# The row of token 512 on GpSimd instead of ScalarE, in an FNet and PEER kernel

## The chip, the core and the metric

The kernel runs on one core of a Trainium2 chip. Its engines run side by side, each in the order of its own queue: TensorE (PE in the profile; its weight loads are PEld), VectorE (DVE), ScalarE (ACT), GpSimd (POOL), and SyncE (SP), whose queue here issues nearly all the DMA transfers. An instruction starts when those before it on its engine have gone ahead and the semaphores that it waits for have come. The time is that of the whole program on the device, in microseconds, and the median of several runs counts. A profile is taken of one execution; it shows every instruction with its start and its length.

## The reference

`x` has 2048 tokens of 512 values. With `xn` the layer norm of `x`, the output is `x + A(xn) + B(xn)`:

```python
# A: Fourier mixing
a = einsum("bsd,ed->bse", x, dft_hid_re)
b = einsum("bsd,ed->bse", x, dft_hid_im)
y = einsum("ts,bse->bte", dft_seq_re, a) - einsum("ts,bse->bte", dft_seq_im, b)
# B: product-key experts, 32 heads, 64 x 64 experts
q = einsum("nd,dhc->nhc", xf, w_q)        # two halves q1, q2 per head
s1, s2 = q1 @ k1.T, q2 @ k2.T             # the best 2 of each, then the best 2 of the 4 sums
g = softmax(top_s); ue, ve = u[top_e], v[top_e]
act = gelu(einsum("nd,nhkd->nhk", xf, ue))
out = einsum("nhk,nhk,nhkd->nd", g, act, ve)
```

## The kernel before

**Stages.** The first 57 us or so hold the layer norm, the sequence transform of part A and the preparation of the query matrices. After them PE works through the scores of part B (line 776), the expert matmuls (905 and 988) and some small products, without using anything of the first stage but its results in memory.

**Groups and folds.** The host has reordered the tokens into four groups `g` of four blocks `q` of 128 tokens, taken in the order `G = (1, 0, 2, 3)`. A transform over 2048 tokens has mirrored columns and rows, so tokens are added to and subtracted from their mirror images before any matmul. `ln(g, n)` normalises group `g`: DVE (or ACT, for the blocks in `onact`) takes mean and variance; ACT takes a square root (316); DVE makes `rstd` and `negm` from it (317 to 321); ACT, and for group 1 DVE too, applies them (333). `fold(k, g)` then folds the group on DVE: `ft` (366), in `fold_d` `ff` and `fo` (348 to 355), and `Q[k][g]` (369, 370). One small copy of `fold_d` is on ACT (353). `main(k, g)` multiplies the DFT matrix by `Q[k][g]` on PE (400) and adds up over the four groups. `k` is 0 for the cosine and 1 for the sine half. `evict(0)` empties the sums of the cosine half out of PSUM (455) and adds the bias `s5c` to the first of them on the way.

**Token 512.** One token is its own mirror image in a way that the blocks have no place for. It is handled as one row on partition 0, `x5`, of two times 512 values:
- line 336 normalises it on GpSimd, when group 0's statistics are there;
- `fold_row(k)` folds it on GpSimd, into `s5` (k = 0) and `s5i` (k = 1), through the row tile `r` of tag `r5` and the same `fold_d`, with GpSimd as engine `e`;
- `spread()` multiplies `s5` by the two values `c52` (385), stores the four rows of 128 in memory and loads them back as columns `s5c` (386, 387: DMAs that GpSimd issues);
- `sides()` adds `s5` times a scalar to two side sums on partition 0 (435 to 438);
- `c52` (514) is a copy of two values of the row `c5r`, which a DMA loads at the start.

**What sets the order.** The program text gives dependences and a first order; each engine's instructions are then put in a queue of their own, by when a scheduler expects their data. So line 435, which stands late in the text, is issued as soon as `s5` is expected. In the queue of ACT the row's operations stand between those of `ln` and `fold`. The two places that the prediction speaks of, in the order of ACT's queue (the number is the line):

```
514 c52 <- c5r, 316 root of group 1, 333 apply x2, 353 copy of the fold of group 1, 297 ... statistics of group 0
333 apply group 0 x4, 353 row copy, 435 row * s5, 296, 385 row * c52 x2, 436 row * c55, 316 root of group 2
```

Of the kernel before, what the change touches and what calls it, by code (L numbers as in the profile page):

```python
# [8 lines left out]
F32 = mybir.dt.float32  # L9
# [6 lines left out]
AF = mybir.ActivationFunctionType  # L16
ALU = mybir.AluOpType
AX = mybir.AxisListType

P = 128  # L20
# [15 lines left out]
def tile_fnet_peer(ctx, tc, x, ca, cb, c5, wt, wf, wr, wq, kt, ut, vn, out):  # L36
# [9 lines left out]
    nc = tc.nc  # L46
# [202 lines left out]
    da = stA.enter_context(tc.tile_pool(name="da", bufs=1, side="left"))  # L249
# [6 lines left out]
    s5 = da.tile([1, 257], F32, name="s5")  # L256
# [9 lines left out]
    def row512(k, dst, eng=nc.sync):  # L266
        eng.dma_start(dst.rearrange("p (k c) -> p k c", k=4),
                      cb[k, 0, 4 * k:4 * k + 4, 0:1, 6:8].rearrange("k p b c -> p k (b c)"))
# [70 lines left out]
    def fold_d(k, t, f, o, e=nc.vector):  # L339

        op, po = (ALU.subtract, ALU.add) if k else (ALU.add, ALU.subtract)

        def halves(v):
            return v.rearrange("p q (s c) -> p q s c", s=2)

        e.tensor_tensor(halves(f)[..., 1:P], halves(t[:, :, 0:256])[..., 0:P - 1],
                          halves(t[:, :, 256:512])[..., 1:P], op=op)
        c = 256 - P * k  # L350
        e.tensor_tensor(o[:, :, c:c + 1], t[:, :, 127:128], t[:, :, 384:385], op=op)
        if k == 0:
            nc.scalar.activation(f[:, :, 0:P + 1:P], t[:, :, 255:257], AF.Copy)
        e.tensor_tensor(o[:, :, k:P], f[:, :, k:P], f[:, :, P + k:], op=op)
        e.tensor_tensor(o[:, :, P + k:2 * P], f[:, :, k:P], f[:, :, P + k:], op=po)

    def fold(k, g):


        op = ALU.subtract if k else ALU.add  # L360
        t = FF["t"] = da.tile([P, 2, 512], F32, tag="ft", name=f"ft{k}_{g}", bufs=1)
        f = None if k else FT.get(G.index(g))
        if f is None:
            f = da.tile([P, 2, 256], F32, tag="ff", name=f"ff{k}_{g}", bufs=2)
        o = FF[k, g] = da.tile([P, 2, 257], F32, tag="fo", name=f"fo{k}_{g}", bufs=2)
        nc.vector.tensor_tensor(t, xp[2 * g], xp[2 * g + 1], op=op)  # L366
        fold_d(k, t, f, o)
        c = slice(k, 257 - k)
        nc.vector.tensor_tensor(Q[k][g][:, 0, c], o[:, 0, c], o[:, 1, c], op=ALU.add)
        nc.vector.tensor_tensor(Q[k][g][:, 1, c], o[:, 0, c], o[:, 1, c], op=ALU.subtract)  # L370

    def fold_row(k):

        r = da.tile([1, 1, 768], F32, tag="r5", name=f"r5_{k}", bufs=1)
        nc.gpsimd.tensor_tensor(r[:, 0, 0:512], x5[:, 0], x5[:, 1], op=ALU.subtract if k else ALU.add)
        fold_d(k, r[:, :, 0:512], r[:, :, 512:768], (s5i if k else s5).unsqueeze(1), nc.gpsimd)

    s5_d = dram.tile([4, P], F32, name="s5_d")
    s5p = da.tile([1, 2, 2, P], F32, name="s5p")
    s5c = da.tile([P, 2, 2], F32, name="s5c")  # L380

    def spread():

        for a in range(2):
            nc.scalar.activation(s5p[:, a].rearrange("o t p -> o (t p)"), s5[:, 0:256], AF.Copy, scale=c52[:, a:a + 1])
        nc.gpsimd.dma_start(s5_d.rearrange("n p -> (n p)").unsqueeze(0), s5p.rearrange("o a t p -> o (a t p)"))
        nc.gpsimd.dma_start(s5c.rearrange("p a t -> p (a t)"), s5_d.rearrange("n p -> p n"), allow_slow_non_contiguous=True)

# [13 lines left out]
    def add(dst, a, v, first=False):  # L402

        if first:
            nc.vector.tensor_scalar(dst, v, a, None, op0=ALU.mult)
        else:
            nc.vector.scalar_tensor_tensor(dst, v, a, dst, op0=ALU.mult, op1=ALU.add)

    def halved(v):
        return v.rearrange("p (k q c) -> p k q c", q=2, k=4)  # L410

    def turned(v):
        return v.rearrange("p (q k c) -> p k q c", q=2, k=4)

    def sides():


        f = FF["t"][:, 0, 0:4]
        nc.vector.tensor_copy(f[:, 0:2], Q[0][G[0]][:, :, 256])
        nc.vector.tensor_copy(f[:, 2:4], c5s[:, :, G[0]])  # L420
        for n, g in enumerate(G):
            for h in range(2):
                a, v = Q[0][g][:, h, 256:257] if n else f[:, h:h + 1], A[0, g][:, h * 512:(h + 1) * 512]
                if n < 3:
                    add(s256[:, h], a, v, n == 0)
                    continue
                for q in range(2):
                    nc.vector.scalar_tensor_tensor(turned(a256[:, h])[:, :, q], halved(v)[:, :, q], a,
                                                   halved(s256[:, h])[:, :, q], op0=ALU.mult, op1=ALU.add)
        for n, g in enumerate(G):  # L430
            for k in range(2):
                add(a5[:, k, :257 - k], c5s[:, k, g:g + 1] if n else f[:, 2 + k:3 + k],
                    Q[k][g][:, k, :257 - k], n == 0)
        r = da.tile([1, 2, 512], F32, name="r256")
        nc.scalar.activation(turned(r[:, 0]), halved(c5r), AF.Copy, scale=s5[:, 256:257])
        nc.scalar.activation(r[:, 1, 0:257], s5, AF.Copy, scale=c55)
        nc.gpsimd.tensor_tensor(a256[0:1, 0], a256[0:1, 0], r[:, 0], op=ALU.add)
        nc.gpsimd.tensor_tensor(a5[0:1, 0], a5[0:1, 0], r[:, 1, 0:257], op=ALU.add)

# [70 lines left out]
    c52 = cst.tile([1, 2], F32, name="c52")  # L510
    c5r = da.tile([1, 512], F32, name="c5r")
    c55 = da.tile([1, 1], F32, name="c55")
    row512(0, c5r, nc.scalar)
    nc.scalar.activation(c52, c5r[:, 0:2], AF.Copy)
    nc.scalar.dma_start(c55, cb[0, 0, 0, 0:1, 8, 0:1])
    for g in G:
        load(1, g)
# [7 lines left out]
    for n, g in enumerate(G):  # L525
        if n < 2:
            ln(g, n)
        if 0 < n < 3:
            ln(G[n + 1], n + 1)
        fold(0, g)  # L530
        if n == 3:
            fold_row(0)
            spread()
            fold_row(1)
        main(0, g)
        if n == 0:
            for t in range(2):
                m_mul(0, t, (2, 3))
            for t in range(2, 4):
                m_mul(0, t, range(KD))  # L540
# [5 lines left out]
    for n, g in enumerate(G):  # L546
# [5 lines left out]
        if n:  # L552
            for q in range(4):
                xpose(4 * G[n - 1] + q, n < 3)
    sides()
    evict(1)
    for q in range(4):
# [754 lines left out]
    with tc.If(rv > 0):  # L1312
        with tc.tile_pool(name="gen", bufs=1) as gp, \
# [10 lines left out]
            def gload(src, shape, tag, name):  # L1324
                t = gp.tile(shape, F32, tag=tag, name=name, bufs=2)
                nc.sync.dma_start(t, src)
                return t

            gx = []
            for i in range(NT):  # L1330
                t = gload(x[i % 4, i // 4], [P, D], "x", f"gx{i}")
                norm(t, t, i)
                gx.append(gsplit(t, [P, D], "xs", f"gxs{i}", bufs=NT))
            for q in range(4):
                ya = gp.tile([P, 4, D], F32, tag="ya", name=f"gya{q}")
                for ri in range(2):
                    pp = [gps.tile([P, 512], F32, tag="gp", name=f"gp{q}{ri}{d}", bufs=4)
                          for d in range(KD)]
                    for i in range(NT):
                        t = gp.tile([P, 512], F32, tag="c", name=f"gc{q}{ri}{i}", bufs=2)  # L1340
# [15 lines left out]
                    for kd, pieces in enumerate((((0, 1, P, 0), (P - 1, 0, 1, 2)), ((0, 1, P, 1), (P - 1, 0, 1, 0)),  # L1356
                                                 ((0, 0, 1, 1), (1, 1, P, 2)), ((0, 0, P, 3),))):
                        t = gp.tile([P, 512], F32, tag="c", name=f"gw{q}{ri}{kd}", bufs=2)
# [3 lines left out]
                    for a in range(4):  # L1362
# [12 lines left out]
                        o = gload(out[b * P:(b + 1) * P], [P, D], "o", f"go{b}")  # L1375
# [54 lines left out]
```

## Time and profile before

| | us |
|---|---|
| median of 3 runs (1165.53 to 1167.51) | 1165.57 |
| the profiled execution | 1163.72 |
| its span, first to last instruction | 1161.9 |
| busy in the span: PE | 1135.6 |
| busy in the span: DVE | 933.6 |
| busy in the span: ACT | 614.6 |
| busy in the span: POOL | 238.2 |

Times inside the execution are counted from the start of the span. In rows of instructions in order of time the columns are start, length, engine, line and operation, then what it writes and reads, the shapes, and how many instructions are merged in the row; the brackets give the engine's idle time before it and what ended it. A row that merges several instructions gives the start of the first and the time that they were busy together. "ACTq" and "SPq" are the queues' own steps, such as issuing a DMA. In rows of windows, each engine has its busy time in that window and, in brackets, the number of instructions; then come the granted clock of PE (1.00 is full), the share of the DMA engines in use and GB/s.

### The profile page before, as it was taken

What the parts mean: (1) busy time and instruction counts of PE and PEld (TensorE: products, weight loads), DVE (VectorE), ACT (ScalarE), POOL (GpSimd) and SP (SyncE); (2) the same over time, 40 slices, a digit from 0 to 9 for tenths busy, and PEclk for the clock granted to TensorE, in tenths of its full rate; (3) what the DMA queues carried; (4) which work ended last, traced back from release to release, by engine and by line L of the source; (5) the groups of instructions that cost most, each with busy time, mean ns of one, the idle gap of its engine ahead of it and who ended that gap; (6) DMA issues with size and microseconds to landing.
All of it is one profiled execution on the core that took longest, in us unless ns stands there. A gap on an engine that the chain in (4) does not pass through costs nothing.

```text
span 1161.9 us, 25370 instructions
## 1 busy us (share of the span) xinstructions
PE 1135.6 (98%) x9930; PEld 724.4 (62%) x9930; DVE 933.6 (80%) x2840; ACT 614.6 (53%) x1063; POOL 238.2 (21%) x226
## 2 busy tenths in 40 slices
PE   5899999999999999999999999999999999999997
PEld 4355555445445449778478469569569559658763
DVE  5987889798998999983994895797886887788670
ACT  4684677777876645354435436436526436334440
POOL 4131455765756420000000010010010000000000
PEclk9899999999999999999999999999999999999999
DMA  9073345233341204261652743644545555451423
GB/s 364 28 265 99 119 132 178 82 146 117 102 146 41 89 25 129 73 217 28 226 174 98 233 157 127 195 163 158 185 158 173 167 173 168 155 170 56 140 74 103
DMA packets 81504, 163.64 MB, mean 141 GB/s; under 512 B 16084, under 2 KB 31323, under 8 KB 81374
## 3 DMA queue, kind: packets, MB, share of 16 engines
q1 hardware_dynamic: 81008, 161.84, 41.7%
q8 instruction: 80, 1.31, 0.5%
q14 instruction: 50, 0.41, 0.1%
q10 hardware_dynamic: 302, 0.08, 0.0%
q0 software_dynamic: 64, 0.00, 0.0%
HBM read 142.69 MB, written 17.63 MB: 138 GB/s over the span
## 4 chain that ended last, share of the span: by engine, by line
PE 94%; DVE 2%; ACT 1%; POOL 1%; DMA 1%; issue 0%; ACTq 0%
PE z L905 29%; PE s L776 29%; PE v L988 28%; PE g L943 4%; PE m L144 2%; PE p L400 2%; ACT xq L333 1%; DMA c5r<-in_cb_dram 1%; PE xp L472 0%; DVE L L933 0%; DVE ft L366 0%; POOL x L336 0%; DVE act L959 0%; DVE w L951 0%; PE hy L485 0%
## 5 line engine op out<-in xcount | busy, mean ns | idle before, releaser
L905 PE MATMUL z<-xb,u 128*128 128x256 f16 (+1 forms) x3840 | 342.7, 251 | 0.0
L988 PE MATMUL v<-v,act 128*128 128x512 f16 x1536 | 338.6, 379 | 0.0
L905 PEld LDWEIGHTS <-u 128*128 128x128 f16 x3840 | 309.7, 98 | 26.4
L776 PE MATMUL s<-m,xq 128*128 128x512 f16 x1344 | 297.3, 379 | 0.0
L988 PEld LDWEIGHTS <-act 128*128 128x128 f16 x1536 | 147.4, 98 | 171.0
L776 PEld LDWEIGHTS <-xq 128*128 128x128 f16 x1344 | 129.5, 98 | 150.4 <-issue 0.2
L933 DVE TENSOR_TENSOR L<-io_lam,cmp 128x2048 f16<-128x2048 f16 x128 | 156.4, 1222 | 57.4 <-PE g L943 57.4
L912 ACT ACTIVATE act<-z,scl 128x256 f32<-128x256 f32 (+1 forms) x224 | 100.7, 498 | 170.1 <-PE z L905 169.9
L784 DVE MAX8 vals<-ss 128x8 f32<-128x64 f32 x1024 | 152.6, 216 | 12.6 <-ACT ss L781 12.3
L1001 POOL TENSOR_TENSOR y<-y,xr 128x512 f32<-128x512 f32 x15 | 25.6, 1707 | 610.8 <-DMA y<-y_d 317.8
L958 ACT ACTIVATE act<-w 128x1024 f16<-128x1024 f32 x52 | 70.0, 1362 | 92.6 <-DVE w L951 91.9
L788 DVE FIND_INDEX8 idx<-vals,ss 128x8 uint16<-128x256 f32 x256 | 107.2, 419 | 0.0
L951 DVE SCALAR_TENSOR_TENSOR w<-act,scl,g 128x1024 f32<-128x1024 f32 x64 | 81.2, 1277 | 29.7 <-ACT act L912 29.7
L1064 ACT ACTIVATE cx<-cx 128x896 f32<-128x896 f32 x64 | 60.5, 946 | 71.9 <-DVE cx L1044 51.4
L781 ACT ACTIVATE ss<-s,wsc 128x512 f32<-128x512 f32 x112 | 74.7, 680 | 44.4 <-PE s L776 34.8
L959 DVE TENSOR_TENSOR act<-w,act 128x1024 f16<-128x1024 f32 x64 | 86.3, 1350 | 4.2 <-ACT act L958 4.2
L1038 DVE TENSOR_TENSOR cx<-cx 128x512 f32<-128x512 f32 (+2 forms) x84 | 48.5, 612 | 26.5 <-DMA cx<-in_cb_dram 22.4
L943 PEld LDWEIGHTS <-L 128*128 128x128 f16 x2048 | 60.6, 96 | 11.2 <-DVE R L941 1.3
L943 PE MATMUL g<-R,L 128*128 128x32 f16 x2048 | 61.7, 176 | 0.3 <-DVE R L941 0.2
L941 DVE TENSOR_TENSOR R<-R,cmp 128x512 f16<-128x512 f16 x128 | 59.0, 461 | 1.5
L166 POOL TENSOR_TENSOR wq<-wq,wh 128x1024 f16<-128x1024 f32 x26 | 55.4, 2131 | 12.1 <-DVE xq L481 7.9
L938 DVE TENSOR_TENSOR R<-io_c,cmp 128x512 f16<-128x512 f16 x128 | 54.9, 429 | 0.0
(291 smaller groups left out, 1088.5 us busy)
## 6 DMA issues: line engine op xcount, KB each, us to landing
v<-v_d SPq DMA_DIRECT2D x67, 512.0 KB, 4.2
cx<-in_cb_dram SPq DMA_DIRECT2D x64, 448.0 KB, 4.2
wq<-in_wq_dram SPq DMA_DIRECT2D x32, 512.0 KB, 6.1
fit<-in_wq_dram SPq DMA_DIRECT2D x28, 512.0 KB, 5.1
uv<-in_vn_dram SPq DMA_DIRECT2D x16, 512.0 KB, 3.8
uv<-in_ut_dram SPq DMA_DIRECT2D x16, 512.0 KB, 6.3
c<-in_ca_dram SPq DMA_DIRECT2D x8, 512.0 KB, 10.3
y<-y_d SPq DMA_DIRECT2D x16, 256.0 KB, 2.6
```

The source lines that it names most:

```text
L776: nc.tensor.matmul(ps, xt[i][:, l, kd, :], m[:, r, kd, :], start=(n == 0), stop=(n == 3 * KD - 1))
L781: nc.scalar.activation(s.rearrange("p g e -> p (g e)"), ps, AF.Copy, scale=inv)
L784: nc.vector.max(vals[:, i, w, :, h], s[:, g, :])
L788: nc.vector.max_index(idx[:, i, w].rearrange("p k h -> p (k h)"), vals[:, i, w, 0:2].rearrange("p k h -> p (k h)"), s[:, w * HC:g + 1, :]. ...
L905: nc.tensor.matmul(ps if n == 1 else ps.rearrange("p (b n) -> p b n", b=2), ug[:, l, c % 2, kd, :], xb2[:, k0, r, kd, :] if n == 1 else xb ...
L912: nc.scalar.activation(ACT[bb][:, cg * m:cg * m + m, :], pv[:, i], AF.Gelu_apprx_tanh, scale=zsc)
L933: nc.vector.tensor_tensor(L.rearrange("p t (l two) -> p t l two", two=2), io_lam.rearrange("p (l two) -> p l two", two=2).unsqueeze(1).to_ ...
L943: nc.tensor.matmul(p[:, hf, t * NC:(t + 1) * NC], L[:, t, :], R[:, t, :], start=True, stop=True)
L951: nc.vector.scalar_tensor_tensor(w, act[:, :, ts], fw, p.rearrange("p h (n c) -> p c (h n)", c=NC), op0=ALU.mult, op1=ALU.mult)
L958: nc.scalar.activation(w16[..., 0], w, AF.Copy)
L959: nc.vector.tensor_tensor(w16[..., 1], w, w16[..., 0], op=ALU.subtract)
L988: nc.tensor.matmul(pv, w16[:, c, :, l], v_sb[g][:, r, cc, :], start=(n + cc == 0 and k == 0), stop=(n == 15 and cc == 1 and k == 2))
```

## The change

All the operations on the row of token 512 that were on ACT go to GpSimd: the copy of `c52` (514), the row's copy in `fold_d` (353, for the row alone), the two scaled rows of `spread` (385) and the two of `sides` (435, 436). The row tile of `sides` is no tile of its own any more but the next user of `fold_row`'s buffer, which is made larger.

```diff
@@ fold_d
         if k == 0:
-            nc.scalar.activation(f[:, :, 0:P + 1:P], t[:, :, 255:257], AF.Copy)
+            if e is nc.gpsimd:
+                e.tensor_copy(f[:, :, 0:P + 1:P], t[:, :, 255:257])
+            else:
+                nc.scalar.activation(f[:, :, 0:P + 1:P], t[:, :, 255:257], AF.Copy)
@@ fold_row
-        r = da.tile([1, 1, 768], F32, tag="r5", name=f"r5_{k}", bufs=1)
+        r = da.tile([1, 1, 1024], F32, tag="r5", name=f"r5_{k}", bufs=1)
@@ spread
         for a in range(2):
-            nc.scalar.activation(s5p[:, a].rearrange("o t p -> o (t p)"), s5[:, 0:256], AF.Copy, scale=c52[:, a:a + 1])
+            nc.gpsimd.tensor_scalar(s5p[:, a].rearrange("o t p -> o (t p)"), s5[:, 0:256], c52[:, a:a + 1], None, op0=ALU.mult)
@@ sides
-        r = da.tile([1, 2, 512], F32, name="r256")
-        nc.scalar.activation(turned(r[:, 0]), halved(c5r), AF.Copy, scale=s5[:, 256:257])
-        nc.scalar.activation(r[:, 1, 0:257], s5, AF.Copy, scale=c55)
+        r = da.tile([1, 1, 1024], F32, tag="r5", name="r256", bufs=1).rearrange("p o (a t) -> p (o a) t", a=2)
+        nc.gpsimd.tensor_scalar(turned(r[:, 0]), halved(c5r), s5[:, 256:257], None, op0=ALU.mult)
+        nc.gpsimd.tensor_scalar(r[:, 1, 0:257], s5, c55, None, op0=ALU.mult)
@@ tile_fnet_peer
     row512(0, c5r, nc.scalar)
-    nc.scalar.activation(c52, c5r[:, 0:2], AF.Copy)
+    nc.gpsimd.tensor_copy(c52, c5r[:, 0:2])
```

Three things follow in the queues of the changed program. ACT loses six instructions and one of the two table loads at its start, and its first statistics of group 0 (297) now stand ahead of the fold copy of group 1 (353). GpSimd's queue becomes: `c52`, `x5`, the first fold with its copy, the two scaled rows of `spread`, the second fold with the first DMA issue (386) after its first operation, the two scaled rows of `sides`, and then the second DMA issue (387). DVE takes the last statistics of group 2 before `ft` of group 0, and the reciprocal for group 2 before a two-element fold operation (351). The queues of PE and SyncE are as before.

## The prediction

> **What bounds the kernel now.** I read the page first, then busy time in two long stretches, then each engine's instructions in order of time up to 57 us.
>
> ```profile
> span 1161.9 us, 25370 instructions
> PE 94%; DVE 2%; ACT 1%; POOL 1%; DMA 1%; issue 0%; ACTq 0%
> ```
> ```profile
> 0.00:57.00 57.00, 37.57 (x117) 21.33 (x118) 42.57 (x117) 30.99 (x67) 16.24 (x31) 0.91 0.54 200
> 57.00:1161.00 1104.00, 1098.06 (x9815) 703.10 (x9814) 891.05 (x2724) 583.65 (x997) 222.00 (x195) 1.00 0.42 138
> ```
> The chain that ended last is TensorE (PE) for 94% of the span. In the second view (window, its length, then busy time of PE, PE's weight loads, DVE, ACT and POOL) PE is busy 1098.06 of the 1104 us after 57, but only 37.57 of the first 57. Nothing that the change touches lies after that, so it can only move the moment from which PE runs without a pause.
>
> ```profile
> 21.27 3.68 PE L148 MATMUL m<-k_sb,wq 128*128 128x64 f32 x32
> 31.74 5.86 PE L400 MATMUL p<-c,q 128*128 128x512 f32 x8 [6.79 <-DVE q L369]
> 44.19 12.87 PE L400 MATMUL p<-c,q 128*128 128x512 f32 x28 [1.72 <-DVE q L369]
> ```
> Each row has start, length, engine, line, operation and, in brackets, the idle time before it. That moment is 44.19: PE waits for the folded blocks `q` of DVE, last for group 3. So I follow what feeds `q`: normalisation on ACT and DVE, then the folds.
>
> ```profile
> 3.92 1.28 ACT L514 ACT_TABLE_LOAD   x1 [3.92 <-issue]
> 8.65 0.20 ACT L514 ACTIVATE c<-c5r 1x2 f32<-1x2 f32 x1 [3.44 <-DMA c5r<-in_cb_dram]
> 8.87 1.28 ACT L316 ACT_TABLE_LOAD   x1
> 10.16 0.30 ACT L316 ACTIVATE sm<-mvs,eps 128x4 f32<-128x4 f32 x1
> 21.74 0.80 ACT L333 ACTIVATE xq<-xq,nm 128x512 f32<-128x512 f32 x1
> 25.08 0.20 ACT L353 ACTIVATE r<-r 1x2 f32<-1x2 f32 x1 [2.53 <-POOL r L375]
> 25.93 0.72 ACT L435 ACTIVATE r<-c5r,s 1x512 f32<-1x512 f32 x1 [0.65 <-POOL s L351]
> 26.76 0.91 ACT L385 ACTIVATE s5p<-s,c 1x256 f32<-1x256 f32 x2
> 27.97 0.28 ACT L316 ACTIVATE ff<-mvs,eps 128x4 f32<-128x4 f32 x1
> ```
> ```profile
> 7.22 0.30 DVE L312 BATCH_NORM_AGGREGATE mvs<-st 128x2 f32<-128x6 f32 x2
> 10.49 0.18 DVE L317 RECIPROCAL sm<-sm 128x4 f32<-128x4 f32 x1 [2.97 <-ACT sm L316]
> 11.29 0.16 DVE L321 SCALAR_TENSOR_TENSOR negm<-mvs,rstd 128x4 f32<-128x4 f32 x1
> 22.57 1.23 DVE L366 TENSOR_TENSOR ft<-xb,xq 128x1024 f32<-128x1024 f32 x1
> 23.83 1.23 DVE L351 TENSOR_TENSOR fo<-ft 128x2 f32<-128x2 f32 x1
> 28.29 0.18 DVE L317 RECIPROCAL ff<-ff 128x4 f32<-128x4 f32 x1 [3.22 <-ACT ff L316]
> 29.38 0.38 DVE L321 SCALAR_TENSOR_TENSOR negm<-mvs,rstd 128x4 f32<-128x4 f32 x1
> 35.24 0.13 DVE L351 TENSOR_TENSOR fo<-ft 128x2 f32<-128x2 f32 x1
> ```
> ACT works in order, and row-512 operations stand twice ahead of a square root that everything waits for. At the start the two-element copy (8.65) waits 3.44 us for a small load, and a second table load follows; the statistics were done at 7.52. Later the row's copy, waiting for GpSimd (POOL), and its scaled rows stand ahead of the root for group 2 (27.97); its last statistics ended near 23.9 (L312 overlaps the L351 row), and DVE then idles 3.22 us.
>
> **The change, part by part.** *First stall.* Without the copy there is one table load, over by 5.20, and the root starts some 0.1 after 7.52: 10.16 becomes 7.6, 2.55 us earlier. What is late next is group 0's data:
>
> ```profile
> 12.28 0.38 SPq L501 DMA_DIRECT2D xq<-in_x_dram  x1
> ```
> ```profile
> SPq L501 <- DMA xb<-in_x_dram: 1.0, 1, 1.0
> ```
> ```profile
> 14.30 0.21 ACT L353 ACTIVATE ff<-ft 128x4 f32<-128x4 f32 x1 [1.29 <-DVE ft L366]
> 14.41 0.62 ACT L297 ACTIVATE q<-xb 128x512 bf16<-128x512 f32 x1
> 15.09 0.43 DVE L354 TENSOR_TENSOR fo<-ff 128x256 f32<-128x256 f32 x1
> ```
> The sync queue waited for `xb` until 12.28, so it landed there. In the changed order ACT's L297, which reads `xb`, stands ahead of L353, which DVE's L354 needs. L353 comes at 12.3 + 0.62 + 0.1 = 13.0 and L354 at 13.25 instead of 15.09. Of 2.55 us 1.85 are kept; that passes on to all of group 0.
>
> *Second stall.* ACT ends group 0's normalisation at 22.54 − 1.85 = 20.7 and, with no row operation ahead, takes the root about 20.9 (its statistics, at 22.6 − 1.85, are there). DVE's L366 runs 20.75 to 22.0 and L317 follows at 22.0 instead of 28.29. L317 to L321 took 0.96 undisturbed (10.49 to 11.45), and a short L351 comes between, 0.13 at its best (35.24): `negm` is done by 23.1 instead of 29.76, **6.65 us earlier**. Group 3, its folds and PE hang on that.
>
> *What it adds.* GpSimd gets two copies and four scaled rows; the row's older GpSimd work stays, but falls on other DVE work.
>
> ```profile
> 19.48 4.22 POOL L336 TENSOR_SCALAR x<-x,mvs,rstd 1x512 f32<-1x512 f32 x2 [4.83 <-DVE rstd L320]
> 23.79 1.26 POOL L375 TENSOR_TENSOR r<-x 1x512 f32<-1x512 f32 x1
> 25.12 0.62 POOL L348 TENSOR_TENSOR r<-r 1x254 f32<-1x254 f32 x1
> 25.87 0.44 POOL L354 TENSOR_TENSOR s<-r 1x128 f32<-1x128 f32 x1
> 33.67 0.83 POOL L387 DMA_DIRECT2D s5c<-s_d  x1 [3.16 <-DMA s_d<-s5p]
> 64.94 4.73 POOL L437 TENSOR_TENSOR u<-u,r 1x512 f32<-1x512 f32 x1 [10.87 <-DVE u L428]
> 111.13 2.86 POOL L165 TENSOR_SCALAR wq<-wq,wsc 128x1024 f32<-128x1024 f32 x1 [10.13 <-ACT wh L158]
> ```
> ```profile
> 23.75:26.76 3.01, 1.20 (x11) 1.06 (x10) 1.32 (x3) 1.02 (x4) 2.86 (x5) 0.85 1.03 412
> 26.76:29.74 2.98, 0.00 (x0) 0.00 (x0) 1.32 (x6) 1.59 (x5) 2.86 (x6) 0.50 0.98 376
> ```
> The windows give the row's two folds on POOL: 2.86 us each (the second count includes the start of a DMA issue). While the first op of the first (23.79 to 25.05) ran, DVE's 128x2 L351 took 1.23 instead of 0.13: two engines reading two operands each exclude one another. It cost nothing then, DVE being about to idle. In the change x5 ends near 17.6 + 4.2 = 21.9, so the same folds fall on DVE's chain and folds of group 2. The price lies between 0 (POOL yields, as L437 did, 4.73 instead of 1.26) and 5.7 (both folds hold DVE throughout). I take 3.0: L375 then L348 ahead of L351 to L321, about 1.1 + 0.5; L354 and L355 ahead of DVE's L348, 0.9; and 0.5 of the second fold, whose L375 (1.26) mostly lies under a one-input L311. That is nearer the middle than either end because DVE's dependent operations leave gaps for POOL, yet its overlapped ones do not.
>
> The new operations have one data input. By L165 an element costs 2.8 ns, by L336 4.1: a 1x256 row 0.7 to 1.05, the 1x512 1.4 to 2.1; with the 1x257 as a 1x256 and the two copies at 0.15 each (ACT's took 0.20), 3.8 to 5.5 in all. I charge DVE nothing for them: L366 at 22.57 took its usual 1.23 inside L336.
>
> The Trainium skill (SBUF — State Buffer, "Who interferes with whom") says instead that a two-input VectorE instruction is excluded by any GpSimd instruction that reads SBUF, for the whole of it; the L351 row agrees, the L366 row does not. By it the new operations would cost too: that is the slower rival below.
>
> The POOL queue holds two DMA issues. The second, L387 (33.67, loading the biases `s5c`), now stands behind the two scaled rows of the side sums. The first issue, L386, comes near 29 and has landed 4 us after its start, as now (its 0.83 of issue and the 3.16 of waiting in the row); the rows are done near 34. L387 starts at 34 to 36 and has landed, by the same 4 us, at 38 to 40.
>
> ```profile
> 45.35 0.87 ACT L455 ACTIVATE u<-p,s5c 128x256 f32<-128x256 f32 x2 [4.03 <-PE p L400]
> ```
> L455 needs it at 45.35 − 3.65 = 41.7, so 1.7 to 3.7 us cover it; beyond that each us of delay costs one, since L455 empties the banks that PE's next matmuls need. The larger row tile in a reused buffer costs nothing: its new user follows the last reader on the same engine.
>
> *Sum.* 6.65 − 3.0 = **3.65 us earlier**. The profiled execution took 1163.72 (span 1161.9, 1.8 around it) and becomes 1160.07. The median of the runs shown, 1165.57, lies 1.85 above it; I forecast for the median: 1165.57 − 3.65 = **1161.9**.
>
> **Rivals.** (a) *POOL yields everywhere*: 6.0 to 6.65 gained, 1159.2. For it L437; against it L351. (b) *Little is kept*: both folds cost 5.7, 0.95 us remains; or PE loses some back at half clock.
>
> ```profile
> 30.00:40.00 10.00, 7.10 (x11) 2.89 (x12) 8.30 (x24) 7.70 (x15) 1.35 (x2) 0.69 0.20 57
> ```
> The granted clock was 0.69 here and eight matmuls took 5.86 after a pause of 6.79. If group 2's block meets a half clock, it runs from 35 to some 41 and group 3 starts about a us late. Either way 0.9 to 2.3 is gained: about 1164. Against it: the first pause on PE gets shorter (25 to 27 instead of 31.7). (c) *Slower: one-input GpSimd work holds DVE.* Place: DVE's chain and folds of group 2, 22 to 33 us. Price: 5.7 for the folds plus at least 3.8 for the new operations against 6.65: 2.85 lost, 1168.4. It decides from 6.65 us of blocking on. For it: GpSimd has more to read just when DVE folds; against it the L366 row. (d) *It does not do what it says*: group 2's root still waits, for its own data. Its loads stand right behind `xb` (12.28) in one queue, and the statistics that read them, unwaited at 19.75 now, would begin at 17.9, 5.6 us after that landing; little chance, about 1164 too, counted in (b).
>
> **How the numbers follow.** Forecast 0.57, (a) 0.17, (b) with (d) 0.17, (c) 0.09. Its own range, with folds at 1.7 to 4.3, is 1160.6 to 1163.2. For 8 in 10 I reach to (a) and over (b): 1159.0 to 1166.0, leaving (c) and some of (a) out. A difference of 0.2% (2.3 us) is about what can be told from none: faster is forecast and (a), 0.74; same is (b), 0.17; slower is (c), 0.09.
>
> **What would show it.** One table load before the first root, the root near 7.6, `q` of group 1 some 1.85 us earlier; the second root near 21 and no ACT wait for POOL ahead of it; DVE's L351 and L318 to L321 lengthened beside POOL's L375 and L348; PE's last pause ending near 40.5 instead of 44.19, and the same spacing after it. I am wrong if that pause ends later than 42, if DVE's folds stretch beside one-input GpSimd rows, if L455 waits for `s5c`, or if PE gains pauses after it.

## The result and the profile after

| | before | after |
|---|---|---|
| median, us (6 runs each) | 1165.55 (1165.27 to 1167.51) | 1161.37 (1159.45 to 1161.95) |
| ratio of after to before | | 0.9958, 95% interval 0.9946 to 0.9971 |
| the profiled execution, us | 1163.72 | 1159.45 |
| its span, us | 1161.9 | 1157.7 |
| busy in the span: PE, DVE, ACT, POOL | 1135.6, 933.6, 614.6, 238.2 | 1136.5, 934.5, 610.6, 245.0 |

The kernel became faster by 4.2 us: 0.5 us more than forecast and inside the range. The lines of the new code stand three further down from line 353 on (333 stays; 354 is now 357, 366 is 369, 375 is 378, 387 is 390, 400 is 403, 455 is 458). In the order of the prediction, first the page's span and its chain of waits, then the busy time in two long stretches:

```profile
span 1157.7 us, 25371 instructions
PE 93%; DVE 3%; DMA 2%; ACT 1%; issue 0%; POOL 0%; SPq 0%; ACTq 0%; POOLq 0%; DVEq 0%
```
```profile
0.00:57.00 57.00, 42.72 (x140) 24.51 (x141) 48.44 (x130) 31.86 (x69) 23.42 (x37) 0.97 0.54 204
57.00:1157.00 1100.00, 1093.73 (x9792) 700.39 (x9790) 886.05 (x2711) 578.74 (x988) 221.56 (x195) 1.00 0.42 138
```

PE is busy 42.72 us of the first 57 instead of 37.57. After that it idles 6.3 us up to 1157, as before (5.9 up to 1161). So the gain arose in the first stage, as the prediction had it. Next the instructions of PE there, and the first eviction:

```profile
26.51 3.70 PE L403 MATMUL p<-c,q 128*128 128x512 f32 x8 [0.45 <-DVE q L372]
34.37 12.04 PE L403 MATMUL p<-c,q 128*128 128x512 f32 x23 [4.16 <-DVE q L372]
```
```profile
40.72 0.87 ACT L458 ACTIVATE u<-p,s5c 128x256 f32<-128x256 f32 x2 [4.16 <-PE p L403]
```

PE's pause of 6.79 us ahead of group 0 has shrunk to 0.45. The one ahead of group 2 grew from about 1 to 4.16 us, and the one ahead of group 3 is gone: its block starts at 39.61 (44.19) without a stop. How PE's waiting is shared out among the groups differs from one execution to the next, with the place where its clock is halved (see the last section): in the second profile of after the three pauses are 2.18, 1.47 and 1.35 us, in the third 1.11, 2.47 and none. The eviction hardly moves (40.72, 40.70 and 40.78). It starts 4.63 us sooner and waits for PE, not for the biases. Now ACT, the first stall and the second:

```profile
3.92 1.28 ACT L316 ACT_TABLE_LOAD   x1 [3.92 <-issue]
7.94 0.30 ACT L316 ACTIVATE sm<-mvs,eps 128x4 f32<-128x4 f32 x1 [2.74 <-DVE mvs L312]
12.01 0.63 ACT L297 ACTIVATE q<-xb 128x512 bf16<-128x512 f32 x1 [1.21 <-DMA xb<-in_x_dram]
12.63 0.19 ACT L356 ACTIVATE ff<-ft 128x4 f32<-128x4 f32 x1
16.17 0.30 ACT L316 ACTIVATE sm<-mvs,eps 128x4 f32<-128x4 f32 x1 [0.76 <-DVE mvs L312]
20.58 0.30 ACT L316 ACTIVATE ff<-mvs,eps 128x4 f32<-128x4 f32 x1
```

One table load is left. The first root waits for its statistics alone and starts at 7.94 (10.16), the root of group 0 at 16.17 (18.28) and that of group 2 at 20.58 (27.97), with no wait of its own. In between, ACT waits 1.21 us for `xb`, as foreseen. Then DVE's chain from the reciprocal to `negm`, for group 2 and for group 3, and what GpSimd did beside it:

```profile
21.61 0.17 DVE L317 RECIPROCAL ff<-ff 128x4 f32<-128x4 f32 x1
21.72 1.23 DVE L351 TENSOR_TENSOR fo<-ft 128x2 f32<-128x2 f32 x1
23.06 0.60 DVE L319 SCALAR_TENSOR_TENSOR ff<-ff 128x4 f32<-128x4 f32 x1
23.89 0.16 DVE L321 SCALAR_TENSOR_TENSOR negm<-mvs,rstd 128x4 f32<-128x4 f32 x1
28.54 1.25 DVE L311 BATCH_NORM_STATS2 ff<-xq 128x6 f32<-128x512 f32 x2
30.43 0.18 DVE L317 RECIPROCAL ff<-ff 128x4 f32<-128x4 f32 x1 [0.43 <-ACT ff L316]
31.72 0.38 DVE L321 SCALAR_TENSOR_TENSOR negm<-mvs,rstd 128x4 f32<-128x4 f32 x1
32.72 0.80 DVE L357 TENSOR_TENSOR fo<-ff 128x256 f32<-128x256 f32 x1
```
```profile
21.68 1.25 POOL L378 TENSOR_TENSOR r<-x 1x512 f32<-1x512 f32 x1
23.01 0.62 POOL L348 TENSOR_TENSOR r<-r 1x254 f32<-1x254 f32 x1
24.00 0.96 POOL L357 TENSOR_TENSOR s<-r 1x128 f32<-1x128 f32 x1
25.66 1.92 POOL L388 TENSOR_SCALAR s5p<-s,c 1x256 f32<-1x256 f32 x2
27.55 2.09 POOL L378 TENSOR_TENSOR r<-x 1x512 f32<-1x512 f32 x1
30.46 0.62 POOL L348 TENSOR_TENSOR r<-r 1x254 f32<-1x254 f32 x1
32.17 1.95 POOL L438 TENSOR_SCALAR r<-c5r,s 1x512 f32<-1x512 f32 x1
35.33 0.87 POOL L390 DMA_DIRECT2D s5c<-s_d  x1
```

L351, which takes 0.13 us alone, ends with POOL's L378 (22.95 and 22.93), and L319 with L348 (23.66 and 23.63). `negm` of group 2 takes 2.44 us from the start of the reciprocal, that of group 3 1.67, where the first group needed 0.97. The links that wait are the ones that the prediction named; what they cost is measured below.

### The profile page after: what moved, and what is told of

Read it like the earlier page. It is cut to its first block, busy times and chain, and to the rows that moved or that the text cites. A ratio compares the mean times of both kernels' runs of the same rounds, so it can differ in the third digit from the quotient of the medians.

```text
span 1157.7 us, 25371 instructions
## 1 busy us (share of the span) xinstructions
PE 1136.5 (98%) x9930; PEld 724.9 (63%) x9930; DVE 934.5 (81%) x2840; ACT 610.6 (53%) x1056; POOL 245.0 (21%) x232
## 4 chain that ended last, share of the span: by engine, by line
PE 93%; DVE 3%; DMA 2%; ACT 1%; issue 0%; POOL 0%; SPq 0%; ACTq 0%; POOLq 0%; DVEq 0%
PE s L779 29%; PE z L908 28%; PE v L991 27%; PE g L946 4%; PE p L403 2%; PE m L144 2%; DVE L L936 1%; PE xp L475 0%; DMA xb<-in_x_dram 0%; DMA x<-in_x_dram 0%; DMA cx<-in_wt_dram 0%; DMA fit<-v_d 0%; DVE act L962 0%; DMA y<-y_d 0%; DVE w L954 0%
## 5 line engine op out<-in xcount | busy, mean ns | idle before, releaser
L1004 POOL TENSOR_TENSOR y<-y,xr 128x512 f32<-128x512 f32 x15 | 25.2, 1679 | 611.9 <-DMA y<-y_d 455.8
```

## The experiments

**How they are read.** The whole time of one kernel varies by some us from run to run, far more than most of these edits are worth. The first stage does not. So two times are taken from each profile: the start of group 0's root (the second L316), and from there to the start of group 3's first fold instruction (`ft` of `k` = 0, L366 or L369). The first holds the stall at the start and the landing of the loads, the second everything that the row costs on the way.

| kernel | group 0's root, us | from it to group 3's `ft`, us |
|---|---|---|
| before | 18.28 | 21.56 |
| before, again | 17.68 | 21.55 |
| after | 16.17 | 18.92 |
| after, again | 16.23 | 18.92 |
| after, a third time | 16.31 | 18.92 |
| only `c52` on GpSimd | 16.49 | 21.17 |
| all but `c52` on GpSimd | 17.76 | 19.10 |
| only the two copies on GpSimd | 16.28 | 21.39 |
| after, `x5` normalised on DVE | 16.07 | 19.38 |
| after, other order on GpSimd | 16.36 | 19.66 |
| after, folds without second operand | 16.01 | 16.97 |
| after, no folds | 16.60 | 16.94 |
| after, no folds, two rows more | 15.69 | 16.93 |

The second column repeats within 0.01 us for the two kernels that ran more than once.

**Are the two stalls separate?** One kernel makes only the `c52` part of the change, the other all the rest.

```diff
 # only c52 on GpSimd (against before)
-    nc.scalar.activation(c52, c5r[:, 0:2], AF.Copy)
+    nc.gpsimd.tensor_copy(c52, c5r[:, 0:2])
 # all but c52 (against after)
-    nc.gpsimd.tensor_copy(c52, c5r[:, 0:2])
+    nc.scalar.activation(c52, c5r[:, 0:2], AF.Copy)
```

> Only the two-element copy of c52 goes to GpSimd; the row's copy and all scaled rows are back on ScalarE. Theory A (two separate stalls in ScalarE's queue, both felt at the end): one table load, the first root near 7.9 as in the changed kernel, group 0 some 2.1 us earlier than before, so the row on GpSimd too; the root of group 2 again stands behind the row copy and a scaled row, which wait for GpSimd until about 23.8, and starts near 24.5 instead of 27.97 (20.58 in the changed kernel). Time 2.1 to 3.2 us below before, about 1162.8. Rival B (the first stall is hidden, all of the gain is in the second): no difference from before, 1165.5.

> The changed kernel with the copy of c52 back on ScalarE. Theory A: two table loads and the first root near 10.2 as before; the root of group 2 near 24.0 (ScalarE ends group 0's normalisation at 22.5 and the copy of group 0's fold now stands ahead), the first reciprocal for group 2 near 24.4 against 28.29 before and 21.61 in the changed kernel. Time 1.5 to 2.1 us below before, about 1163.7. Rival B (first stall hidden): as the changed kernel, 1161.4.

Measured beside 26 runs of before with a median of 1166.22: with `c52` alone 1163.16 (ratio 0.9971, 0.9959 to 0.9984), with the rest alone 1163.49 (0.9981, 0.9969 to 0.9992). The medians lie 0.4 and 0.2 us from what theory A expected. The second ratio alone would not show a gain, since the unchanged kernel differs from itself by nearly as much (0.9985, below); the first stage does. In the table the first moves only group 0's root (1.79 us) and 0.39 of the second column, the second kernel only the second column (2.46 us), apart from when the loads land. The first stall is felt at the end of the stage too: with `c52` alone the first eviction comes at 43.16 us, 1.6 to 2.2 us sooner than in the two profiles of before (44.73 and 45.35). So rival B falls. This view shows the queue of ACT with `c52` alone moved; the row's operations are still ahead of group 2's root:

```profile
23.28 0.20 ACT L356 ACTIVATE r<-r 1x2 f32<-1x2 f32 x1 [2.54 <-POOL r L378]
24.14 0.72 ACT L438 ACTIVATE r<-c5r,s 1x512 f32<-1x512 f32 x1 [0.65 <-POOL s L351]
24.77 0.28 ACT L316 ACTIVATE ff<-mvs,eps 128x4 f32<-128x4 f32 x1
```

The root starts at 24.77 instead of 20.58, after two waits for GpSimd, while its statistics had ended at 20.86. The first root of the other kernel starts at 9.53, behind the copy and two table loads.

**Is it the copy or the scaled rows that hold the second root?** The copies stay on GpSimd; the scaled rows go back to ACT (this diff and those that follow are against after).

```diff
-            nc.gpsimd.tensor_scalar(s5p[:, a].rearrange("o t p -> o (t p)"), s5[:, 0:256], c52[:, a:a + 1], None, op0=ALU.mult)
+            nc.scalar.activation(s5p[:, a].rearrange("o t p -> o (t p)"), s5[:, 0:256], AF.Copy, scale=c52[:, a:a + 1])
...
-        nc.gpsimd.tensor_scalar(turned(r[:, 0]), halved(c5r), s5[:, 256:257], None, op0=ALU.mult)
-        nc.gpsimd.tensor_scalar(r[:, 1, 0:257], s5, c55, None, op0=ALU.mult)
+        nc.scalar.activation(turned(r[:, 0]), halved(c5r), AF.Copy, scale=s5[:, 256:257])
+        nc.scalar.activation(r[:, 1, 0:257], s5, AF.Copy, scale=c55)
```

> The changed kernel with the four scaled rows (spread and sides) back on ScalarE; both copies stay on GpSimd. Theory A (the place in ScalarE's queue decides, not ScalarE's load): a scaled row that waits for the whole first fold stands ahead of the root of group 2, which starts near 25.5 instead of 20.58, and negm of group 2 ends near 27 against 24.05 changed and 29.76 before: 1 to 2 us above the changed kernel. Rival C (the copy that waits for GpSimd was the stall, the scaled rows are only load): root near 21, as the changed kernel within 0.7 us.

A single execution took 1163.55 us. In the queue of ACT:

```profile
25.00 0.51 ACT L388 ACTIVATE s5p<-s,c 1x256 f32<-1x256 f32 x1 [4.46 <-POOL s L358]
25.41 0.28 ACT L316 ACTIVATE ff<-mvs,eps 128x4 f32<-128x4 f32 x1
```

The wait only moved on: the scaled row waits 4.46 us for the end of the fold on GpSimd, and the root comes at 25.41. Moving the row's copy beside `c52` gains nothing (21.39 against 21.17). Every operation of the row that stands ahead of the root has to go; the wait is for GpSimd's folds, whatever reads them.

**What do the folds on GpSimd cost DVE?** Three kernels take away parts of it, one adds more of what the rival suspects.

First, `x5` is normalised on DVE, so that the first fold starts 3 us sooner:

```diff
-                nc.gpsimd.tensor_scalar(x5[:, q], x5[:, q], mvs[0:1, 0, q + 2, 0:1], rstd[0:1, 0, q + 2:q + 3],
+                nc.vector.tensor_scalar(x5[:, q], x5[:, q], mvs[0:1, 0, q + 2, 0:1], rstd[0:1, 0, q + 2:q + 3],
```

> The changed kernel with the normalisation of x5 on VectorE (two instructions of 1x512) instead of GpSimd (4.2 us). Theory A (what is left of the cost is that GpSimd's two-input folds shut VectorE out on its chain for group 2): VectorE pays about 1.0 us ahead of group 2's statistics, the first fold falls at 19 to 22 us under one-input statistics, and the chain from the reciprocal to negm shrinks from 2.44 to about 1.1 us; net 0.3 to 0.8 us below the changed kernel, about 1160.9. Rival D (no such exclusion): 1.0 us above it, 1162.4.

The chain of group 2, now clear of the first fold, takes 1.03 us instead of 2.44, as it should. Still, the expected 0.3 to 0.8 us did not come: the median is 1162.21 (ratio 0.9967, 0.9951 to 0.9982), no better than after, and group 3's `ft` comes 0.46 us later. The two rows themselves take DVE 0.98 us ahead of the chain, and two more of its rows show the rest:

```profile
24.82 1.40 DVE L357 TENSOR_TENSOR fo<-ff 128x256 f32<-128x256 f32 x1
29.78 1.19 DVE L369 TENSOR_TENSOR ft<-xq,xq 128x1024 f32<-128x1024 f32 x1
```

The second fold, sooner too, now falls on group 2's folds (L357 takes 1.40 instead of 0.43), and in the new order of DVE's queue three statistics of group 3 stand ahead of `ft` of group 2 (29.78; 27.32 in after). The collision was moved, not removed.

Second, no folds at all on GpSimd:

```diff
-        nc.gpsimd.tensor_tensor(r[:, 0, 0:512], x5[:, 0], x5[:, 1], op=ALU.subtract if k else ALU.add)
-        fold_d(k, r[:, :, 0:512], r[:, :, 512:768], (s5i if k else s5).unsqueeze(1), nc.gpsimd)
+        nc.gpsimd.tensor_copy(s5i if k else s5, x5[:, k, 0:257])
```

> The row's two folds are left out: each is one copy of 257 elements, so its values are those of one half of the row. Theory A: the two-operand instructions of the folds on GpSimd hold VectorE, 1.35 us on group 2's chain and 0.7 on group 3's. Without them negm of group 2 is done near 22.75 (24.05 in the changed kernel) and that of group 3 near 30 to 30.4 (32.09), PE's last wait and the first eviction come 1.5 to 2.3 us sooner (38.4 to 39.2), and the time is 1.5 to 2.3 us below the changed kernel. Rival B: the chain is slow for another reason (the order of VectorE's queue, the memory); then nothing moves by more than 0.4 us. Rival C: any GpSimd instruction that reads holds VectorE, one operand or two; then the copies and the scaled rows, which now fall on the same chain, take back most: negm of group 3 no earlier than 31.5.

Third, the folds keep every instruction, but each has one operand (`one(d, v)` is a `tensor_scalar` on GpSimd; five of them, with the same shapes, stand for the two-operand ones):

```diff
-        nc.gpsimd.tensor_tensor(r[:, 0, 0:512], x5[:, 0], x5[:, 1], op=ALU.subtract if k else ALU.add)
+        one(r[:, 0, 0:512], x5[:, k])
...
```

> Every two-operand instruction of the row's folds on GpSimd becomes a one-operand one of the same shape, at the same place in the queue: the sums and differences in the row's values are left out. GpSimd is then as busy as before or more (a 512-element row 1.95 instead of 1.25). Theory A: what holds VectorE is the second operand, so the two long rows of group 2's chain go, L351 1.23 and L319 0.60, down to 0.2 to 0.5 each, and negm of group 2 comes at 22.8 to 23.5 instead of 24.05. Rival C: it is the whole length of any reading GpSimd instruction; then the chain is as long or longer, negm of group 2 at 24.0 to 25. The eviction is not read, since the row ends later on GpSimd.

Fourth, the kernel without folds gets two long one-operand rows:

```diff
...
+            for _ in range(2):
+                nc.gpsimd.tensor_scalar(junk5, x5[:, 0], c52[:, 0:1], None, op0=ALU.mult)
```

> As the kernel without folds, with two more one-operand rows of 512 elements on GpSimd (about 1.9 us each, into a tile that nobody reads) among its scaled rows, between 24 and 32 us, where VectorE runs two-operand folds nearly without a pause. Theory A: a one-operand instruction of GpSimd keeps VectorE out only while it reads, about 0.37 us for 512 elements by the 0.80 instead of 0.43 of one VectorE row, so negm of group 3 comes 0 to 0.8 us later than in the kernel without folds. Rival C: it keeps two-operand VectorE instructions out for its whole length; then 3.9 us of rows cost 2.5 to 3.9 us there, and single VectorE rows of 0.43 take up to 2.3. The eviction is not read here, since the biases' second transfer is pushed back by the same rows.

The kernel without folds has a median of 1159.17 over four runs (ratio 0.9953, 0.9936 to 0.9969, to a median of 1164.71 of before; after itself in the same session 1161.85 and 0.9973). Its first `negm` values missed the expected 22.75 (23.22), since the loads landed 0.4 us later in that execution. Counted from the reciprocal, the chain of group 2 takes 1.18 us (2.44), and from there to `negm` of group 3 it is 7.32 us (8.04): 1.26 and 0.72 us less, 1.98 together. The table has the same, 16.94 against 18.92, and the eviction starts at 39.09. Single executions of the other two took 1162.58 and 1158.35 us; what counts is their first stage. First two rows of DVE without folds, then DVE and GpSimd with one-operand folds, then DVE and GpSimd with the two rows more (their code lines differ):

```profile
22.04 0.17 DVE L317 RECIPROCAL ff<-ff 128x4 f32<-128x4 f32 x1
22.98 0.24 DVE L321 SCALAR_TENSOR_TENSOR negm<-mvs,rstd 128x4 f32<-128x4 f32 x1
```
```profile
21.55 0.55 DVE L351 TENSOR_TENSOR fo<-ft 128x2 f32<-128x2 f32 x1
22.21 0.16 DVE L319 SCALAR_TENSOR_TENSOR ff<-ff 128x4 f32<-128x4 f32 x1
...
21.42 1.56 POOL L381 TENSOR_SCALAR r<-x,c 1x512 f32<-1x512 f32 x1
23.07 1.10 POOL L381 TENSOR_SCALAR r<-r,c 1x254 f32<-1x254 f32 x1
```
```profile
25.55 1.20 DVE L371 TENSOR_TENSOR ft<-xq,xq 128x1024 f32<-128x1024 f32 x1
...
23.68 1.60 POOL L540 TENSOR_SCALAR junk<-x,c 1x512 f32<-1x512 f32 x1
26.12 2.06 POOL L540 TENSOR_SCALAR junk<-x,c 1x512 f32<-1x512 f32 x1
```

With one-operand folds GpSimd is busier than in after, its first row 1.56 us instead of 1.25, and still L351 is released after 0.55 us, a little over the 0.2 to 0.5 expected, and L319 not held at all. The two further rows cost nothing (16.93): DVE's `ft` keeps its 1.20 us, and it is GpSimd's row that takes 2.06 instead of 1.60. So rival C, that any reading instruction of GpSimd holds DVE for its length, falls, and with it the slower rival of the prediction. What holds DVE is the second operand on both sides: the two statistics of DVE that run beside GpSimd's second long two-operand row in after (L311 at 28.54) take 1.25 us, as they do without folds. The price of the second operand is 1.95 us (18.92 against 16.97), that of the whole folds 1.98. The one-operand instructions are also of another kind, `tensor_scalar` instead of `tensor_tensor`; the runs do not tell the kind from the number of operands.

The one-operand kernel shows one thing more. Its row ends later on GpSimd, and the eviction then waits for the biases:

```profile
38.28 0.86 POOL L400 DMA_DIRECT2D s5c<-s_d  x1
...
41.04 0.87 ACT L468 ACTIVATE u<-p,s5c 128x256 f32<-128x256 f32 x2 [6.60 <-DMA s5c<-s_d]
```

They were there 2.76 us after the start of that issue. In after, the issue starts at 35.33; by the same 2.76 us, an estimate, they were there near 38.1, 2.6 us ahead of the eviction at 40.72.

**Does it matter which operations of GpSimd stand where?** The same instructions as in after, with the first scaled row of the side sums called right behind `spread()`, ahead of the second fold:

```diff
             spread()
+            r = FF["r256"] = da.tile([1, 2, 512], F32, name="r256")
+            nc.gpsimd.tensor_scalar(turned(r[:, 0]), halved(c5r), s5[:, 256:257], None, op0=ALU.mult)
             fold_row(1)
...
```

> The changed kernel with the same instructions on GpSimd in another order: the first scaled row of the side sums comes before the last two additions of the first fold, and the second before the last two of the second fold. Theory A: only two-operand instructions hold VectorE for their length, and it matters what lies beside them. Then the second fold's last two additions (0.44 each) leave group 3's root and negm and come beside group 2's last folds, ahead of a pause of 0.43 us on VectorE that takes most of them. From the reciprocal of group 3 to the end of negm it then takes 1.2 to 1.4 us instead of 1.67, group 3's ft comes 0.2 to 0.6 earlier, counted from the first root, and the time is 0 to 0.6 us below the changed kernel (0.3% to 0.4% below before). Rival B: the price goes with GpSimd's busy time, whatever its instructions; the order then changes nothing, group 3's ft stands within 0.15.

The order matters, so rival B falls, but it went the other way: 19.66 instead of 18.92, and a median of 1162.81 (ratio 0.9968, 0.9955 to 0.9981) beside 1161.64 of after. Two rows of DVE:

```profile
30.20 0.77 DVE L351 TENSOR_TENSOR fo<-ft 128x2 f32<-128x2 f32 x1
31.89 0.52 DVE L319 SCALAR_TENSOR_TENSOR ff<-ff 128x4 f32<-128x4 f32 x1
```

The second fold's first addition (1.25 us) had given way to DVE's `ft` in after (2.09 us) and then run beside one-operand statistics, which cost DVE nothing. The delayed queue put it at 29.69, beside L351, behind which the last of group 3's statistics is queued; and its next (0.62) came at 31.76, on the chain again. So group 3's root comes 0.87 us later than in after, counted from group 0's, while its chain from the reciprocal to `negm` shrinks only from 1.67 to 1.54 us, not to the 1.2 to 1.4 expected. The expectation had followed the last two additions and overlooked the first.

**How large is the gain?** After again, twice, and before again, unchanged:

> The changed kernel once more, beside the next three. By its first runs it stands 0.42% (0.29 to 0.54) below the kernel before, some 3.5 to 6 us. If the first stage sets the gain and the rest of the program only scatters, its profile shows group 2's negm again near 24.05 (5.7 earlier than before), group 3's near 32.1 and the first eviction near 40.7, each within 0.3, whatever the whole time does. If the gain was partly an accident of that execution, these times move by more.

> The changed kernel a third time, for the size of the gain. Its two first stages were alike within 0.1 us after 16 us, PE 4.63 us ahead of before from 54 us on, but the ratios were 0.9958 and 0.9973. If the rest of the program only scatters, 10 or more runs give a ratio between 0.996 and 0.9975 (2.9 to 4.6 us) and PE is again 4.4 to 4.8 ahead at 55 us. If the gain hung on the execution, PE's lead there moves by more.

> The kernel before, unchanged. Ratio 1 within 0.1%. If the first stage is as repeatable before as after, PE stands within 0.4 us of the first profile at 55 us and after, and any further difference up to the end arises at single places in the part after 57 us, as in the profiles of the changed kernel.

| | median, us | before beside it | ratio |
|---|---|---|---|
| after, again | 1161.85 (10 runs) | 1164.71 | 0.9973, 0.9963 to 0.9984 |
| after, a third time | 1161.64 (10 runs) | 1166.07 | 0.9958, 0.9944 to 0.9972 |
| before, again | 1164.63 (10 runs) | 1166.07 | 0.9985, 0.9972 to 0.9998 |

The unchanged kernel missed its expected 0.1%: it differs by 0.15% from its own runs, so a ratio is no surer than that. The third ratio of after, 0.9958, lies just outside the expected 0.996 to 0.9975. Over all sessions 26 runs of after have a median of 1161.5 and 72 of before one of 1166.0 (1165.7 with the ten of before, again). The first stage came out as expected: PE is 4.63, 4.64 and 4.55 us ahead of the first profile of before at 55 us. The second profile of before is itself 0.61 ahead, which was not expected either: `c5r` landed 0.8 us sooner in it.

```profile
7.86 0.20 ACT L514 ACTIVATE c<-c5r 1x2 f32<-1x2 f32 x1 [2.56 <-DMA c5r<-in_cb_dram]
9.37 0.30 ACT L316 ACTIVATE sm<-mvs,eps 128x4 f32<-128x4 f32 x1
```

So the first stall is worth 1.4 to 2.1 us, by how late `c5r` comes. And after 57 us single places take back a part, another one each time. First a wait in the second profile of after; then the third profile's windows (PE's clock follows the five busy times), beside the same window in the first:

```profile
1054.85 2.84 PE L908 MATMUL z<-xb,u 128*128 128x128 f16 x48 [1.24 <-ACT act L915]
```
```profile
103.00:107.00 4.00, 4.00 (x16) 1.46 (x14) 0.14 (x1) 0.78 (x2) 0.00 (x0) 0.64 0.00 0
```
```profile
103.00:107.00 4.00, 4.00 (x24) 1.79 (x22) 1.86 (x12) 2.54 (x8) 0.50 (x1) 1.00 0.00 0
```

Ahead of 1054.85 PE had waited 1.24 us for ACT; from 103 to 107 us its clock was 0.64 of full speed on the average, and 1.4 us went. In the first profile of after PE's lead shrank by only 0.4 us from 55 us to the end of the program.

## Why the prediction was right

- **What bounds it.** Right: the gain is PE's earlier end of waiting in the first stage. After 57 us PE idles as little as before (6.3 and 5.9 us).
- **First stall, 1.85 us.** Right in mechanism, a little small: 2.11 us at group 0's root. One table load, the root as soon as its statistics are there (7.94, not 7.6, as they ended at 7.91 in this execution), then the wait for `xb`, which landed near 12.0 and not 12.28. Against the second profile of before it would be 1.5; the landing of `c5r` is part of the number. By the rows of before the copy ended 1.33 us behind the statistics (8.85 and 7.52) and the second table load took 1.28 more; no run takes the two apart.
- **Second stall, the reciprocal of group 2 at 22.0.** It came at 21.61, 6.68 us sooner (6.3 forecast). Both halves were tested alone, and the copy alone is not enough.
- **Contention, 3.0 us.** The term that was mis-sized: 1.98 us, near the lower end of its own 1.7 to 4.3. The 1.6 for L378 and L348 on group 2's chain measured 1.26 and the 0.5 for the second fold 0.72. The 0.9 for L354 and L355 beside group 2's folds was not there: from `negm` to the next `ft` it is 3.27 us in after and 3.24 without folds. There it was mostly GpSimd that waited (L357 on POOL took 0.96 us, 0.44 alone).
- **The new operations at nothing for DVE.** Nearly right. After's L357 took 0.80 instead of 0.43 beside a one-operand row, so single instructions are held, which the prediction had named as a sign of being wrong. The size is small: from `negm` of group 2 to the next `ft` it is 2.99 us in before and 3.24 without folds, where one such row stands beside DVE. Two further one-operand rows left the path as it was.
- **The biases.** The second issue was forecast for 34 to 36 and came at 35.33. Their cover is 2.6 us; the forecast had 1.7 to 3.7.
- **PE's last pause.** Off, though by the execution: not near 40.5 but at 34.37, and at 39.48 in the second profile of after. In the first the half clock of rival (b) came, after the pause of 4.16 us, and let group 2's block run until group 3's data were there. It cost about 0.1 us, not the 1 us of the rival, because the block still had 5 us to run in: the lead over before is 4.75 us at group 3's `ft` and 4.63 at the eviction, and 4.69 and 4.65 in the second profile, where group 2's block ran at full clock.
- **The sum.** 2.11 + 2.64 (21.56 − 18.92) − 0.12 − 0.4 in the rest of the program = 4.2 us, against 1.85 + 1.80 = 3.65. The loss in the rest was not in the sum; against the first profile of before it is 0.4 to 2.5 us in those of after, and the second of before loses 1.1 us there too, so the runs do not charge it to the change. The close fit owes something to luck: the two stalls gave 0.26 and 0.84 us more than forecast, the half clock and the rest of the program took 0.12 and 0.4 that the sum did not have, and with the rest as in the second profile of after only some 2.1 us would have been left.
- **The rivals.** (a), GpSimd yielding everywhere, would have given 6.0 or more; the folds do cost 1.98. (b), little kept, does not hold: the folds cost 1.98 and not 5.7, and the half clock about 0.1. (c), slower, fell with the two further rows. (d) did not happen: the second root waits for nothing.

Open: whether an earlier first stage makes the clock's dip near 103 us likelier. Five of the eleven profiles with some part of the change show one and neither of the two of before. The change need not be the cause. In all five the dip begins a whole number (20 to 23) of lengths of 3.41 us after a fall of the clock in the first stage of the same execution, and the length that ends there holds 2.65 to 2.95 us of a stretch in which PE multiplies by only one or two columns (lines 568 to 578 of after, 2.95 us). In the eight profiles without a dip no such length holds more than 2.12 us of that stretch. So the dip goes with where those lengths lie in an execution.

## What to carry to other kernels

On an engine that works in order, a two-element copy is not small: its price is the wait that it brings to what stands behind it, here 3.4 us for a load and 2.5 to 4.5 for another engine's folds. When such work is moved, all of it that stands ahead of the critical instruction must go, and what it meets in its new place is to be looked up instruction by instruction: two-operand work of GpSimd beside short two-operand instructions on a chain of DVE costs much of its own length (1.26 us for the 1.87 of two instructions on group 2's chain), one-operand work beside the same chain costs next to nothing (16.97 us against 16.94 without folds). Compare a stage with itself, from one event to another, where the whole program scatters by more than the edit is worth.

## What the runs showed of the hardware

**Two operands against one.** A two-operand GpSimd instruction held a two-operand DVE instruction until its end (L351 1.23 us instead of 0.13). The other way round, GpSimd's rows gave way to DVE's `ft`: 2.09 us instead of 1.25 for one with two operands, 2.06 instead of 1.60 for one with one. A one-operand GpSimd instruction of 1.95 us delayed a DVE instruction by only 0.37 (0.80 instead of 0.43), less than 1 ns for each of its 512 elements. The Trainium skill (SBUF — State Buffer, "Who interferes with whom") has it that whichever of a two-input VectorE instruction and a reading GpSimd instruction starts first keeps the shared ports for its whole length. The traces agree for two-operand GpSimd work and not for one-operand work: with 3.66 us more of it the stage took 16.93 us, as without it (16.94).

**The clock of PE** fell for a set time, 3.41 us or two or three times that, in each of the thirteen profiles. In the first profile of after it was 0.50 in the second of these windows, behind the pause of 4.16 us, and full on both sides.

```profile
31.00:35.20 4.20, 0.83 (x2) 0.49 (x3) 3.59 (x10) 2.93 (x4) 4.10 (x6) 1.00 0.24 93
35.20:38.60 3.40, 3.40 (x5) 1.35 (x4) 3.33 (x6) 0.21 (x1) 1.00 (x2) 0.50 0.06 1
38.60:42.00 3.40, 3.40 (x9) 1.52 (x8) 3.40 (x9) 1.28 (x3) 0.00 (x0) 1.00 0.00 0
```

In before it was 0.50 from 25.9 to 36.1 us, 10.2 us or three times 3.4, and in the second profile of after from 25.2 to 32.0, two times. The Trainium skill (TensorE: Matmul & The Clock Gate, "Part 1: The HAM clock gate (the "warmup" mystery)") gives a free-running window of some 3.4 us for this, which these lengths bear out. The fall has no fixed place behind a pause. In the windows above it came 0.8 us after the pause of 4.16 us had ended, so the pause was paid for in the work behind it, free where that work has slack, as here; in before it came 0.9 us after the pause of 6.79 us had begun. In the second profile of after it fell on group 0's block, and those of groups 2 and 3 ran at full clock:

```profile
34.43 3.70 PE L403 MATMUL p<-c,q 128*128 128x512 f32 x8 [1.47 <-DVE q L372]
39.48 12.93 PE L403 MATMUL p<-c,q 128*128 128x512 f32 x28 [1.35 <-DVE q L372]
```
